# A new order of steps in the down stages of an mLSTM cell with a GELU feed-forward

## The chip, the cores and the metric

The kernel runs on one core of one Trainium2 chip. The metric is the device time of one execution in microseconds (us). Its engines are TensorE (PE), VectorE (DVE), ScalarE (ACT), GpSimd (POOL) and SyncE (SP), which here issues nearly all DMAs.

## The reference

Two parts follow each other. The first is a recurrent cell over 768 time steps for 4 batches and 8 heads of 40 elements; the second is a feed-forward block with exact GELU on the cell's output, 3072 rows of 320.

```python
for t in range(S):                                   # S = 768
    m_new = np.maximum(f_gate[:, :, t] + m, i_gate[:, :, t])
    f_stab = np.exp(f_gate[:, :, t] + m - m_new)
    i_stab = np.exp(i_gate[:, :, t] - m_new)
    m = m_new
    C = f_stab[..., None, None] * C + i_stab[..., None, None] * np.einsum('bhd,bhe->bhde', vt, kt)
    n = f_stab[..., None] * n + i_stab[..., None] * kt
    h_tilde = np.einsum('bhde,bhe->bhd', C, qt)
    denom = np.maximum(np.abs(np.einsum('bhd,bhd->bh', n, qt)[:, :, None]), 1.0)
    y[:, :, t] = sigmoid(o_gate[:, :, t]) * h_tilde / denom
x = y.transpose(0, 2, 1, 3).reshape(B * S, H * D)    # 3072 x 320
h = x @ w_in                                         # 320 x 2048
out = (0.5 * h * (1.0 + erf(h / sqrt(2)))) @ w_out   # 2048 x 320
```

## The kernel before

The sequence is cut into six chunks of 128 steps, numbered from 0. Within a chunk the cell becomes matmuls: scores of queries and keys times a matrix of decays, plus the state that the chunks before left. The feed-forward block of a chunk (512 rows: four batches of 128) has an up part (with GELU) and a down part.

The order of the work is written out by hand, as a string of words that `play` runs from left to right. Each word is a letter and batch numbers, and calls one Python function that emits instructions; each engine then runs its own instructions in that order, and an engine that has to wait holds all that is behind it on that engine. The string `FRONT` covers the start up to chunk 0's down part. The string `DOWN` is played once for each of the chunks c = 1 to 4: it mixes the down part of chunk c with the cell of chunk c+1. Between two plays of `DOWN` stands `up`, which is the same each time. Chunk 5's down part is written separately.

```python
steps = cell_steps(c + 1, "MWGTscVYXRLKQDCBSjh", g)
steps |= dict(F=in_turn(products), Z=in_turn(fourth[-1:]), N=late)
play(DOWN, steps)
```

The letters of `DOWN` mean this (b is a batch; numbers are lines):

- F: the next of 14 products of the down part (L1137). Each is 8 matmuls of 128x128 by 128x160 in full float32, which the trace shows as 16 matmul records. Seven results are made by two F each; after the second, the result leaves its bank: p1 (L1152) and p2 (L1158) by a ScalarE copy, p6, p5, p7, p3 and p4 by a VectorE addition (L1148). Two banks take turns.
- Mb, Wb: mask (POOL, L439) and exponential (ScalarE, eight of L465) of the matrix of decays W of batch b. Gb: the output gate (ScalarE sigmoid, L475). The exponential and the sigmoid lie in different activation tables, so a change between them puts a table load on ScalarE.
- S0, S2: the scores of batches 0 and 1, or 2 and 3 (TensorE, L557), and their multiplication with W (VectorE, eight of L563). C0, C2: what the state gives to the same two batches (L612). h0, h2: the state's update (TensorE L623, VectorE L632 and L638, POOL L636).
- Vb: the values (TensorE, L659) and their addition (VectorE, L667).
- Kb, Qb: VectorE transposes of keys and queries (L491) from blocks that a DMA brought. L3 clears and loads the block of batch 3 (POOL memsets L481, SP L167). D3: POOL product L528. B3: SP load of the last W. j: SP loads of the next chunk's first block (L167) and 16 copies from DRAM to DRAM (L159).
- Yb: the end of batch b (L674 to L688: ScalarE, POOL, VectorE) and, where its turn has come, a copy (L695). Xb: three transposes on TensorE into a bank px (L706) and a ScalarE copy (L716). Rb: two VectorE operations on px (L729, L730), after which the bank is free. Two px banks take turns.
- N: two VectorE subtractions (L1163) that the eleventh F and later ones need. Z: two VectorE subtractions of weights (L846), only in the first play.

```python
def sum_late():                                       # N
    for i in range(2):
        a12 = g.t[:, HF + HF // 2 * i:HF + HF // 2 * (i + 1), 0:HT]
        nc.vector.tensor_tensor(out=a12, in0=a12, in1=g.s2[i], op=OP.subtract)
```

Of the kernel before, what the change touches and what calls it, by code (L numbers as in the profile page):

```python
# [30 lines left out]
    M3 f2 S2 V1 Y0 T3 J Y1 C2 j8 W3 j9 e K K K J S3 J C3 f3 K X0 B8 J K R0 B9 h5 J h6 h7 K J V2 K Y2 J J Z Z K  # L31
    K V3 X1 J K r F J h8 h9 F F K F F F F F J K X2 G3 F F J K J F J K Y3 K B10 R1 X3 F p R2 J R3 F F J F F"""
DOWN = """
    M0 F Z F L3 W0 M1 W1 S0 C0 F F h0 Q2 F K2 G1 D3 B3 V0 G2 M2 W2 M3 W3 V1 K3 Q3 F G0 S2 Y0 G3 C2 h2 F
    F Y1 X0 V2 V3 F N F j R0 Y2 Y3 X1 F F X2 R1 F R2 X3 R3 F"""


@with_exitstack
# [1231 lines left out]
```

## Time and profile before

| what | value |
|---|---|
| median of 3 runs | 455.32 us (453.95 to 457.4) |
| the profiled execution | 455.19 us |
| its span, first to last instruction | 453.3 us |
| TensorE busy | 444.2 us (98%) |
| VectorE, ScalarE, POOL busy | 314.7, 238.2, 77.3 us |
| granted TensorE clock | 1.00 |
| DMA traffic | 51.12 MB, 113 GB/s over the span |
| TensorE's instruction transfers (queue q8) | 43 packets, 0.70 MB |

The profile is one execution. Busy times are unions of an engine's instructions; ends of matmuls are modelled, so TensorE can be shown busy while it makes less progress than it could. In a timeline line the first figure is the start in us, the second the duration of the merged group, and a bracket at the end names idle time ahead of it and what ended it. In a line that begins with a stretch A:B, the length comes first and then, for each engine, its busy time and number of instructions, the granted clock, the share of the DMA engines and GB/s. [...]

### The profile page before, as it was taken

The page shows a single profiled execution, that of the slowest core. Times are in us where ns is not written, and L with a number is a line of the kernel's source. Part 1 is how long each engine was busy: PE and PEld are TensorE (multiplying, and loading weights), DVE is VectorE, ACT ScalarE, POOL GpSimd, SP SyncE. Part 2 cuts the span into 40 slices and gives each one's busy share as a digit, 9 for nine tenths or more (in the row PEclk, how much of TensorE's full clock was granted, in tenths as well). Part 3 has the DMA queues.
Part 4 walks back from the last instruction along what each step waited for, and adds up shares of the span by engine and source line. Part 5 has one row for each costly group of instructions (what it writes and reads, how often), then busy time and mean ns, then how long its engine had stood idle before and what let it go on. Part 6 is the DMA issues. An engine that isn't in the chain of part 4 may idle for free.

```text
span 453.3 us, 13140 instructions
## 1 busy us (share of the span) xinstructions
PE 444.2 (98%) x5440; PEld 393.2 (87%) x5440; DVE 314.7 (69%) x672; ACT 238.2 (53%) x541; POOL 77.3 (17%) x117
## 2 busy tenths in 40 slices
PE   8899999999999999999999999999999999999996
PEld 7787888777788999988999988899988899988996
DVE  8797688877269688735578656488645577699940
ACT  4999999764231791221791203693203594247701
POOL 3002030000100443101433101533001513000000
PEclk9999999999999999999999999999999999999999
DMA  7999874886265644149834139942019930200001
GB/s 156 235 211 229 191 212 88 240 246 162 75 153 124 108 63 111 45 92 212 137 55 111 45 57 221 126 88 23 25 47 208 151 81 4 88 30 0 1 1 59
DMA packets 174876, 51.12 MB, mean 113 GB/s; under 512 B 154752, under 2 KB 168352, under 8 KB 174816
## 3 DMA queue, kind: packets, MB, share of 16 engines
q1 hardware_dynamic: 174496, 49.95, 50.5%
q8 instruction: 43, 0.70, 0.6%
q10 hardware_dynamic: 320, 0.33, 0.2%
q14 instruction: 17, 0.14, 0.1%
HBM read 45.47 MB, written 10.03 MB: 122 GB/s over the span
## 4 chain that ended last, share of the span: by engine, by line
PE 88%; ACT 6%; DVE 2%; DMA 1%; SPq 1%; issue 1%; DVEq 0%; ACTq 0%
PE po L1137 27%; PE pu L1021 23%; PE po L1116 8%; PE pu L1032 6%; PE po L991 6%; PE ph L659 3%; PE ps L557 3%; ACT W L465 2%; PE pu L810 2%; PE pf L612 2%; PE px L706 2%; PE pu L877 2%; PE pf L623 1%; SPq L151 1%; DMA bits<-in_moe_w_in_dram 1%
## 5 line engine op out<-in xcount | busy, mean ns | idle before, releaser
L1036 ACT ACTIVATE g<-pu 128x512 f32<-128x512 f32 x64 | 32.2, 618 | 81.2 <-PE pu L1032 81.2
L1137 PE MATMUL po<-w_out,g 128*128 128x160 f32 x512 | 74.4, 302 | 0.0
L1137 PEld LDWEIGHTS po<-w_out,g 128*128 128x128 f32 x512 | 70.1, 190 | 1.9 <-ACT g L1036 1.3
L1021 PE MATMUL pu<-x_hi,w_in_hi 128*128 128x512 f32 x160 | 39.0, 387 | 0.0
L465 ACT ACTIVATE W<-W,aT 128x128 f32<-128x128 f32 x128 | 38.6, 388 | 0.1
L439 POOL TENSOR_SCALAR_AFFINE_SELECT W<-W 128x1024 f32<-128x1024 f32 (+2 forms) x20 | 25.0, 1254 | 77.9 <-DMA W<-M_d 77.3
L1137 PE MATMUL po<-w_sums,sums 128*128 128x160 f32 x256 | 36.9, 302 | 0.0
L1137 PEld LDWEIGHTS po<-w_sums,sums 128*128 128x128 f32 x256 | 35.0, 190 | 0.4
L1116 PE MATMUL po<-w_out,g 128*128 128x320 f32 x128 | 34.9, 432 | 0.0
L1021 PEld LDWEIGHTS pu<-x_hi,w_in_hi 128*128 128x128 f32 x160 | 29.5, 189 | 5.7 <-ACT g L1036 1.3
L1116 PEld LDWEIGHTS po<-w_out,g 128*128 128x128 f32 x128 | 24.1, 190 | 9.7
L563 DVE TENSOR_TENSOR W<-ps,W 128x256 f32<-128x256 f32 (+1 forms) x48 | 18.1, 416 | 18.3 <-PE ps L557 7.1
L1021 PE MATMUL pu<-x_all,w_mid 128*128 128x512 f32 x80 | 30.3, 379 | 0.0
L1021 PE MATMUL pu<-x_all,w_in_mid 128*128 128x512 f32 x80 | 30.3, 379 | 0.0
L528 POOL TENSOR_TENSOR vw<-vb,ewT 128x328 f32<-128x328 f32 x12 | 9.2, 777 | 114.3 <-DMA vb<-in_v_dram 71.8
L864 DVE TENSOR_TENSOR sums<-g 128x512 f32<-128x512 f32 x16 | 12.8, 801 | 21.8 <-ACT g L1036 21.8
L384 DVE SCALAR_TENSOR_TENSOR pow<-sig,pow 128x320 uint32<-128x320 uint32 (+1 forms) x26 | 15.5, 597 | 7.2 <-ACT pow L373 7.2
L695 ACT COPY y_rest<-ob 128x128 f32<-128x128 f32 x16 | 4.7, 294 | 29.3 <-DVE ob L688 21.1
L372 ACT ACTIVATE sig<-bits 128x320 f32<-128x320 f32 (+1 forms) x26 | 15.1, 582 | 9.2 <-DMA bits<-in_moe_w_out_dram 4.4
L1021 PE MATMUL pu<-x_lo,w_in_lo 128*128 128x512 f32 x80 | 18.9, 379 | 0.0
L1021 PE MATMUL pu<-x_lo,w_in 128*128 128x512 f32 x80 | 18.9, 379 | 0.0
L1137 PE MATMUL po<-t,g 128*128 128x160 f32 x128 | 18.7, 299 | 0.0
(220 smaller groups left out, 960.8 us busy)
## 6 DMA issues: line engine op xcount, KB each, us to landing
W<-M_d SPq DMA_DIRECT2D x16, 512.0 KB, 5.2
bits<-in_moe_w_in_dram SPq DMA_DIRECT2D x20, 256.0 KB, 4.8
bits<-in_moe_w_out_dram SPq DMA_DIRECT2D x16, 320.0 KB, 4.5
blocks<-kq_d SPq DMA_DIRECT2D x32, 128.0 KB, 3.6
ob<-in_o_gate_dram SPq DMA_DIRECT2D x24, 160.0 KB, 4.6
out_dram<-o_sb SPq DMA_DIRECT2D x36, 80.0 KB, 1.9
kq_d<-in_k_dram SPq DMA_DIRECT2D x32, 80.0 KB, 2.4
kq_d<-in_q_dram SPq DMA_DIRECT2D x32, 80.0 KB, 2.5
```

The lines of the kernel that those rows point to most:

```text
L372: nc.scalar.activation(out=s, in_=hi.bitcast(F32), func=AF.Copy, scale=2.0 ** -112)
L384: nc.vector.scalar_tensor_tensor(out=p, in0=s, scalar=3, in1=p, op0=OP.logical_shift_left, op1=OP.bitwise_or)
L439: nc.gpsimd.affine_select(out=x, in_=x, compare_op=OP.is_ge, fill=1.0e30, base=base, pattern=[[0, H], [1, x.shape[2]]], channel_multiplier=-1)
L465: nc.scalar.activation(out=W[n][:, h, :], in_=src, func=AF.Exp, scale=-1.0, bias=aT[:, self.c, r:r + 1])
L557: nc.tensor.matmul(ps[i][hip][halves[x ^ i], p, t], kT[i][r, p, halves[x]], qT[i][r, p, t], start=True, stop=True)
L563: nc.vector.tensor_tensor(out=w[r, :, t], in0=ps[i][hip][r, :, t], in1=w[r, :, t], op=OP.mult)
L991: nc.tensor.matmul(in_pairs(po[t]), x[:, t * L:(t + 1) * L], in_turns(w), start=(f, k) == first, stop=(f, k) == last, skip_group_check=True)
L1021: nc.tensor.matmul(in_pairs(pus[i][e]), w[k][:, e, i * P:(i + 1) * P], in_turns(x[:, k, :]), start=(n == 0 and k == 0), stop=False, skip_g ...
L1032: nc.tensor.matmul(in_pairs(pu[e]), w[r, i // 2, i % 2 * P:(i % 2 + 1) * P], in_turns(x[r, NX, :]), start=False, stop=(n == 2), skip_group ...
L1036: nc.scalar.activation(out=g.t[:, HF * e + i, :], in_=pu[e], func=AF.Gelu, scale=4097.0)
L1116: nc.tensor.matmul(po[b], g.t[:, f, b * L:(b + 1) * L], w_out[:, f, :], start=(f == 0), stop=(f == NF - 1))
L1137: nc.tensor.matmul(bank[k][:, t, :], lhs(j, t), rhs(j), start=(first and t == 0 and j == 0), stop=(t == 1 and j == HF - 1), skip_group_che ...
```

## The change

The string `DOWN` is put in another order. It has the same words; nothing else in the program differs.

```diff
 DOWN = """
-    M0 F Z F L3 W0 M1 W1 S0 C0 F F h0 Q2 F K2 G1 D3 B3 V0 G2 M2 W2 M3 W3 V1 K3 Q3 F G0 S2 Y0 G3 C2 h2 F
-    F Y1 X0 V2 V3 F N F j R0 Y2 Y3 X1 F F X2 R1 F R2 X3 R3 F"""
+    L3 G1 M0 F W0 M1 F K2 W1 S0 C0 B3 F F M2 Z h0 Q2 D3 V0 V1 W2 F M3 W3 G2 G0 F j Q3 K3 S2 Y0 C2 h2 G3 F F Y1
+    X0 V2 V3 N F Y2 R0 X1 F Y3 X2 R1 R2 F X3 R3 F F F"""
```

Seen from TensorE the steps stand as follows (words of other engines left out):

```
before  F F S0 C0 F F h0 F V0 V1 F S2 C2 h2 F F X0 V2 V3 F F X1 F F X2 F X3 F
after   F F S0 C0 F F h0 V0 V1 F F S2 C2 h2 F F X0 V2 V3 F X1 F X2 F X3 F F F
```

On the other engines: L3 and G1 come first, ahead of the first mask and exponentials; K2 comes ahead of the second exponentials; the gates G2 and G0 stand together behind the last exponentials; M2, Z, B3 and j move; N stands ahead of the ninth F, and R0 ahead of X1.

## The prediction

> **What bounds the kernel now.** I read the busy table first, then the busy time of each engine in the four stretches that the change touches, then TensorE's and VectorE's timelines of one of them, and last the packets of the instruction queues.
>
> ```profile
> PE 444.2 (98%) x5440; PEld 393.2 (87%) x5440; DVE 314.7 (69%) x672; ACT 238.2 (53%) x541; POOL 77.3 (17%) x117
> q8 instruction: 43, 0.70, 0.6%
> 147.41:190.09 42.68, 42.57 (x814) 41.10 (x813) 32.34 (x70) 23.85 (x60) 16.29 (x22) 1.00 0.44 85
> 216.79:260.06 43.27, 42.70 (x814) 41.09 (x813) 31.42 (x68) 23.85 (x60) 15.13 (x22) 1.00 0.46 85
> 286.75:329.55 42.80, 42.68 (x814) 41.09 (x813) 31.36 (x68) 23.86 (x60) 14.44 (x21) 1.00 0.36 57
> 356.25:396.69 40.44, 40.39 (x751) 39.37 (x749) 29.48 (x60) 23.95 (x61) 12.67 (x15) 1.00 0.33 64
> ```
>
> The last four lines are the down stages that run beside the cells of chunks 2, 3, 4 and 5 (I call them stages 2 to 5): length, then TensorE's busy time and its matmul records. TensorE has almost no idle time, at full clock. An order can only win what these stages lose beyond their matmuls. But a busy figure hides short waits, because ends are modelled, so I measured each step from start to start.
>
> ```profile
> 221.33 1.57 PE L557 MATMUL ps<-qT,kT 64*64 64x128 f32 x64
> 223.74 4.61 PE L1137 MATMUL po<-w_sums,sums 128*128 128x160 f32 x32
> 229.03 2.44 PE L1137 MATMUL po<-w_out,g 128*128 128x160 f32 x16
> 231.40 1.67 PE L659 MATMUL ph<-vb,W 128*32 128x41 f32 x128
> 233.00 2.44 PE L1137 MATMUL po<-w_out,g 128*128 128x160 f32 x16
> 235.37 1.84 PE L557 MATMUL ps<-qT,kT 64*64 64x128 f32 x60
> 244.54 0.71 PE L659 MATMUL ph<-vb,g 128*32 128x41 f32 x52
> 245.76 0.34 PE L659 MATMUL ph<-vb,g 128*32 128x41 f32 x12 [0.51 <-issue]
> ```
>
> Two losses show in stage 3. Scores and reads (S0 C0) take 223.74-221.33 = 2.41 us the first time. The second time (S2 C2, to L623 at 238.16) they take 2.79; in stage 2 it is 3.04, in stage 4 2.96, in stage 5 2.41. And 52 records into the last batch of values TensorE stops: 0.71 us from start to start, released by nothing but issue. VectorE says why S2 is slow:
>
> ```profile
> 232.26 0.71 DVE L491 STREAM_TRANSPOSE qT<-blocks 128x512 f32<-128x512 f32 x1
> 232.89 0.67 DVE L491 STREAM_TRANSPOSE kT<-blocks 128x512 f32<-128x512 f32 x1
> 233.59 0.91 DVE L667 TENSOR_TENSOR far<-ph,far 128x328 f32<-128x328 f32 x2
> 234.41 0.70 DVE L491 STREAM_TRANSPOSE kT<-blocks 128x512 f32<-128x512 f32 x1
> 235.04 0.67 DVE L491 STREAM_TRANSPOSE qT<-blocks 128x512 f32<-128x512 f32 x1
> ```
>
> K3 and Q3 end at 235.71, when S2 has already begun (235.37); its matmuls of the second batch wait for them.
>
> **The change, part by part.** Times with a plus count from the start of stage 3 (216.79). No instruction is added except waits; 4 of ScalarE's 28 table loads go, and TensorE has 3 wait instructions fewer.
>
> (a) *Products beside each other.* F after other matmuls costs more than F after F: 16 records alone take 231.40-229.03 = 2.37, twice 4.74, while the pair at 216.79 takes 4.54. Behind h0 the order F, V0 V1, F becomes V0 V1, F F: 0.20 less in stages 2 to 4. In stage 5, 6.72+2.37 become about 4.45+4.54: 0.10. The tail has as many pieces as before. Sum -0.7, bounds -0.9 and -0.3.
>
> (b) *The wait in S2.* Now K2 comes ahead of the score multiplies, where VectorE sat idle 2.1 us for ScalarE, so one transpose (0.67) leaves the queue ahead of K3. G1 goes ahead of W0: ScalarE ends the gelus at +2.18, then table load 1.28, gate 0.47, load 1.28, so W0 starts at +5.3 (it was +6.4), the copy of p1 (0.43) comes between W0 and W1, and W1 ends at +10.4 instead of +11.2. K3 and Q3 so end 0.67+0.7 sooner, at +17.5. TensorE reaches S2 at +18.25 (h0 ends at +12.24, values 1.47, F F 4.54). The wait falls away with 0.7 to spare; in stage 2 the weight sums that Z moved behind W1's multiplies take 0.55 of that. Of the excess of 1.56 in all, 0.27 (stages 2 and 4) lies in the C2 part and is not this wait. I take -1.2; bounds -1.3 and -0.6.
>
> What else moves is covered. POOL's two memsets of L3 (0.94 each, from +0.0, held until the up stage has read x_lo) now stand ahead of mask M0, which ends near +3.0; W0 needs it at +5.3. The p1 copy is 3 us later; its bank is next written by the fifth F, at +13.7. The p2 copy waits for W3 (mask M3 ends near +15.3, exponentials to +17.9, load 1.28, gates 0.83, copy 0.40: +20.4), and the seventh F wants that bank at +21.4: 1.0 to spare. On SP, the 20 issues of j stay held by Q2 as before (233.67 to 249.52), and the sends behind them begin at 255.92. B3 keeps its place on SP between L3's loads and those of V0. The table load that goes (1.28 per stage) lies on ScalarE, busy 23.9 of 43.
>
> (c) *Instruction transfers.* In the packet records the 16 KB packets of q8 come once in 256 TensorE instructions (43 for some 10,975). In the stop the packet moved from 243.18 to 244.33, TensorE went on at 245.76, 1.43 after its end, and the next packet began at 247.57. So a block that nothing runs ahead of costs a cycle of 4.39; the closest two starts are 3.43 apart (162.54, 165.97). The stop marks a block's start; from there I count 256 at a time, each F being 32 instructions, V0 V1 256, h0 64, S0 C0 256. By step rows, the blocks of the new order that run short are: stage 3, from the end of the F F behind C0 through h0 into V1, 0.74+1.1 = 1.9 us (it was 4.1, with an F inside); stage 3, the last F into V3, 2.4 (was 2.65, the one that stopped); stage 5, F into V1, 2.6 (was 4.6); stage 2, into C2, 2.7 as before; stage 4, 3.7 as before, and one of 2.2 becomes 4.2. The 1.9 looks worst, but its transfer is asked for while slow products are still queued: in the trace the packet there began at 226.97, ended at 228.12, plus 1.43 is 229.55, and TensorE needs the block at 223.74+4.54+0.74+1.1 = 230.1. The V3 stop stays: that block and the one ahead of it sum to 7.9 in both orders. I take 0.7 there and 0.5 elsewhere, against about 1.0 now: +0.2, bounds -1.0 and +6.7 (below).
>
> The Trainium skill, "Runtime: NRT & Kernel Launch", section "Instruction fetch mechanics", gives TensorE room for 2048 instructions, so that the cost of a boundary is mostly hidden. The stop at 245 speaks against it; by it this term would be zero in both kernels and the sum -1.6.
>
> (d) *The px banks.* X1 and X2 now stand one F earlier, N still ahead of them on VectorE. From V3's end: the add of L667 and N take until +3.1 (246.03 to 249.11 in the trace), reciprocal and gate product to +3.8, R0's two operations to +4.75; only then is X0's bank free for X2, whose place on TensorE is F, X1, F = 2.27+0.33+2.20 = +4.8. X3 behind R1 comes out as level. No slack: I take 0.1 in three stages, +0.3; bounds 0 and +3.6 (0.9 in each stage, as when L866 took 1.58 instead of 0.68 beside a POOL mask).
>
> Sum: -0.7-1.2+0.2+0.3 = -1.4. The profiled execution took 455.19 (span 453.3 and 1.9 around it), the median is 455.32; the forecast is 453.9 by either.
>
> **The rivals.** *All transfers hide* (0.20): the V3 stop goes too and nothing new waits: -0.7-1.3-1.0 = -3.0, 452.3. For it: blocks ahead of the short ones grow (stage 2, 3.2 to 5.2); against it: the 7.9 above. *The banks decide* (0.14): N's length puts X2 and X3 behind, about 0.45 to 0.9 a stage: -1.7+1.8 to -1.7+3.6, 455.4 to 457.2. For it: VectorE's operations stretch beside POOL; against it: POOL has one short product there. *A transfer is not asked for early* (0.09, the slower side): if a request goes out only when TensorE itself begins the block, the short blocks cost 4.39 less their length: 2.5, 2.0, 1.8, 1.7 and 0.7, 8.7 in all, against 1.0 now. With (a) and (b) that is +5.8: 461.1. It decides once the block of 1.9 has its transfer later than 0.6 us behind today's place. For it: fast blocks are packed closer; against it: the start at 226.97, 0.8 ahead of TensorE's own crossing. *The order does nothing* (0.05): another operation, such as the masks, holds K3 and Q3, and the time stays at 455.3.
>
> **How the numbers follow.** The forecast has 0.52, with its own range of 452.9 to 455.0. The range 452.0 to 456.6 adds the first rival, the last, and the lower half of the banks. Over 1% is 4.6 us, about what a measurement of this kernel tells from no change. All that these stages lose is 3.3 us, so faster by over 1% has 0.04, for what I cannot see; slower by over 1% has 0.10, the third rival and a little; the rest, 0.86, is within.
>
> **What would show it.** Stage lengths of about 42.2, 42.8, 42.4 and 40.5; S2 C2 at 2.4 in all; K3 and Q3 ending ahead of S2; a stop left in V3 of stage 3. A stop in V0 V1 of stage 3 over 0.5 us means (c) is wrong; X2 or X3 starting later than the end of the F ahead of it means (d). A stage over 43.3 makes the forecast wrong.

## The result, and the profile after

The changed kernel is slower: 459.53 us in the median of 8 runs (458.28 to 461.33) against 456.31 for the kernel before in the same session (8 runs, 453.95 to 457.4). The ratio (of the means) is 1.0086, with a 95% interval of 1.0058 to 1.0113. The profiled execution took 459.5 us with a span of 457.4. I had forecast 453.9 and a range that ended at 456.6: the sign was wrong.

The first line below is the busy table of the profile after; the others are the four down stages, in the same view and columns as those shown of before (length, then busy time and number of records of TensorE, its weight loads, VectorE, ScalarE and POOL, then clock, DMA share and GB/s).

```profile
PE 444.8 (97%) x5440; PEld 393.1 (86%) x5440; DVE 321.8 (70%) x672; ACT 232.8 (51%) x537; POOL 82.3 (18%) x117
148.09:191.75 43.66, 42.81 (x814) 41.02 (x813) 34.55 (x70) 22.48 (x59) 18.56 (x23) 1.00 0.43 83
218.45:262.44 43.99, 42.72 (x814) 40.94 (x813) 33.18 (x68) 22.48 (x59) 17.38 (x23) 1.00 0.44 84
289.15:331.60 42.45, 42.16 (x815) 40.81 (x813) 32.15 (x68) 22.46 (x59) 18.66 (x22) 1.00 0.35 58
358.25:400.75 42.50, 40.86 (x749) 39.44 (x748) 30.24 (x60) 26.80 (x69) 13.17 (x16) 1.00 0.35 69
```

Three things are to be seen. The stages sum to 172.60 us instead of 169.19, so 3.4 of the 4.1 us by which the span grew lie in them. The up stages between them last 26.69 us in both kernels, and what follows the last one 56.6; the rest lies ahead of the first stage, where the programs are alike and where the first stage began anywhere between 147.4 and 149.3 us in the profiles of this study. From here on I therefore compare sums of the four stages, and medians only beside them. Second, TensorE's idle time grows (43.99-42.72 = 1.3 us in stage 3, 1.6 in stage 5). Third, VectorE has *more* busy time (33.18 instead of 31.42 in stage 3), though it has the same 68 instructions.

Measured from start to start and added up over the four stages, TensorE's steps come to this:

| step of the prediction | forecast | measured |
|---|---|---|
| (a) F, up to V3 | -0.7 | -0.6 |
| (b) S0 C0 and S2 C2 | -1.2 | -0.9 |
| (c) values V (instruction transfers) | +0.2 | +2.0 |
| (d) from V3 on: X, F (px banks) | +0.3 | +2.95 |
| sum | -1.4 | +3.4 |

The gains came; two losses are far larger than I had them. TensorE's timeline of stage 3 shows both:

```profile
229.95 0.81 PE L623 MATMUL pf<-vw,kb 128*40 128x41 f32 x32
230.69 1.32 PE L659 MATMUL ph<-vb,W 128*32 128x41 f32 x91
232.51 0.57 PE L659 MATMUL ph<-vb,W 128*32 128x41 f32 x37 [0.50 <-issue]
...
250.07 2.34 PE L1137 MATMUL po<-w_out,g 128*128 128x160 f32 x16
252.65 0.41 PE L706 MATMUL px<-ident,ob 128*128 128x128 f32 x2 [0.24 <-DVE x_all L730]
...
253.01 2.34 PE L1137 MATMUL po<-w_out,g 128*128 128x160 f32 x16
255.67 0.41 PE L706 MATMUL px<-ident,ob 128*128 128x128 f32 x2 [0.32 <-DVE x_all L730]
```

V0 V1 stop after 91 records for nothing but issue (0.70 us from start to start; in stage 5, 1.32). X2 and X3 wait for L730, the second operation of R0 and R1, which empties their bank: F, at 2.18 us otherwise, takes 252.65-250.07 = 2.58 and 255.67-253.01 = 2.66 until the transposes start. In the kernel before, X3 follows its F without a wait:

```profile
255.49 2.34 PE L1137 MATMUL po<-t,g 128*128 128x160 f32 x16
257.67 0.38 PE L706 MATMUL px<-ident,ob 128*128 128x128 f32 x2
```

The timelines of POOL, VectorE and SP in stage 3 show what stands behind the first stop. The sums of the up stage's results (L864 to L866, hidden work of VectorE) now run beside all four instructions of the three masks M0 to M2 (POOL, L439), where only the two of M1 ran before. After the change:

```profile
220.44 5.66 POOL L439 TENSOR_SCALAR_AFFINE_SELECT W<-W 128x1024 f32<-128x1024 f32 x4
```
```profile
221.02 1.58 DVE L866 TENSOR_TENSOR g<-g 128x512 f32<-128x512 f32 x1
222.52 1.57 DVE L864 TENSOR_TENSOR sums<-g 128x512 f32<-128x512 f32 x1
224.12 1.02 DVE L865 TENSOR_TENSOR sums<-sums,g 128x512 f32<-128x512 f32 x1
225.07 1.57 DVE L866 TENSOR_TENSOR g<-g 128x512 f32<-128x512 f32 x1
```
```profile
226.79 0.38 SPq L184 DMA_DIRECT2D g<-M_d  x1
```

The same in the kernel before:

```profile
218.77 2.69 POOL L439 TENSOR_SCALAR_AFFINE_SELECT W<-W 64x1024 f32<-64x1024 f32 x2
```
```profile
219.36 1.58 DVE L866 TENSOR_TENSOR g<-g 128x512 f32<-128x512 f32 x1
220.86 1.13 DVE L864 TENSOR_TENSOR sums<-g 128x512 f32<-128x512 f32 x1
222.03 0.69 DVE L865 TENSOR_TENSOR sums<-sums,g 128x512 f32<-128x512 f32 x1
222.64 0.69 DVE L866 TENSOR_TENSOR g<-g 128x512 f32<-128x512 f32 x1
```
```profile
223.47 0.38 SPq L184 DMA_DIRECT2D g<-M_d  x1
```

B3's load (L184: 512 KB) waits for them, because its target is freed by them. It was issued at 223.47-216.79 = +6.7 of the stage and is now issued at 226.79-218.45 = +8.3. The packet of 16 KB that holds the end of V0 V1 began, by the packet records, at +10.18 before (226.97). Now it begins at 230.24, +11.8, as the burst of B3's load fades (DMA engines full from 228.2 to 229.5), it ends at 231.22, and TensorE goes on 1.29 us later.

My theory: (1) the tail loses 2.9 us to the px banks, because N and the end of batches 2 and 3 stand ahead of R0 and R1 on VectorE while X2 and X3 have moved forward; (2) V0 V1 lose 2 us because the masks slow the sums, the sums delay B3's load, and that load's burst delays an instruction packet. The rival to (2): the stops come simply from putting h0, V0 and V1, all fast work, next to each other. The rival to (1): N, or the chain that ends batches 2 and 3, holds the tail wherever X2 stands.

### The profile page after: what moved, and what is told of

It reads as the page before. It is cut to its first block, busy times and chain, and to the rows that moved or that the text cites. A ratio compares the mean times of both kernels' runs of the same rounds, so it can differ in the third digit from the quotient of the medians.

```text
span 457.4 us, 13122 instructions
## 1 busy us (share of the span) xinstructions
PE 444.8 (97%) x5440; PEld 393.1 (86%) x5440; DVE 321.8 (70%) x672; ACT 232.8 (51%) x537; POOL 82.3 (18%) x117
## 4 chain that ended last, share of the span: by engine, by line
PE 74%; issue 11%; DVE 7%; ACT 5%; POOL 2%; DVEq 0%; POOLq 0%; ACTq 0%
PE pu L1021 23%; PE po L1137 19%; PE po L1116 8%; PE po L991 6%; PE pu L1032 6%; PE ph L659 3%; PE pu L810 2%; PE ps L557 2%; DVE g L1163 2%; ACT W L465 2%; PE pf L612 1%; PE px L706 1%; POOL ob L679 1%; ACT g L1036 1%; PE pu L877 1%
## 5 line engine op out<-in xcount | busy, mean ns | idle before, releaser
L439 POOL TENSOR_SCALAR_AFFINE_SELECT W<-W 128x1024 f32<-128x1024 f32 (+2 forms) x20 | 27.7, 1398 | 55.5 <-DMA W<-M_d 40.0
L528 POOL TENSOR_TENSOR vw<-vb,ewT 128x328 f32<-128x328 f32 x12 | 9.1, 771 | 117.9 <-DMA vb<-in_v_dram 30.2
L864 DVE TENSOR_TENSOR sums<-g 128x512 f32<-128x512 f32 x16 | 14.6, 910 | 21.8 <-ACT g L1036 21.8
L1148 DVE TENSOR_TENSOR o_sb<-po,o_sb 128x320 f32<-128x320 f32 x20 | 9.8, 491 | 18.5 <-PE po L1137 18.3
L481 POOL MEMSET blocks<- 32x1024 f32 x8 | 7.6, 945 | 74.7 <-PE pu L1032 74.5
L372 ACT ACTIVATE sig<-bits 128x320 f32<-128x320 f32 (+1 forms) x26 | 15.1, 581 | 10.2 <-DMA bits<-in_moe_w_out_dram 6.3
L1021 PE MATMUL pu<-x_lo,w_in_lo 128*128 128x512 f32 x80 | 18.9, 379 | 0.0
```

The lines of the kernel that those rows point to most:

```text
L372: nc.scalar.activation(out=s, in_=hi.bitcast(F32), func=AF.Copy, scale=2.0 ** -112)
L439: nc.gpsimd.affine_select(out=x, in_=x, compare_op=OP.is_ge, fill=1.0e30, base=base, pattern=[[0, H], [1, x.shape[2]]], channel_multiplier=-1)
L864: nc.vector.tensor_tensor(out=s1, in0=a21, in1=a22, op=OP.add)
L1021: nc.tensor.matmul(in_pairs(pus[i][e]), w[k][:, e, i * P:(i + 1) * P], in_turns(x[:, k, :]), start=(n == 0 and k == 0), stop=False, skip_g ...
```

## The experiments

Each edit is of the string `DOWN` of the changed kernel unless said; only the words around it are shown. "Sum" is that of the four stages in one profile (before 169.19, changed 172.60). The sizes of stops differ between profiles: the three kernels with the same words up to V3 (changed, old tail, N behind R0) stop in V0 V1 for 0.70, 0.42 and 0.71 us in stage 3 and for 1.32, 1.32 and 1.60 in stage 5. So a difference of 0.3 us between two sums shows nothing by itself.

| kernel | sum, against before | ratio to before (95%) |
|---|---|---|
| changed | +3.4 | 1.0086 (1.0058 to 1.0113) |
| masks moved | +2.1 | 1.0043 (1.0023 to 1.0063) |
| old tail | -0.3 | 1.0018 (0.9994 to 1.0041) |
| an F back between h0 and V0 | +2.3 | 1.0050 (1.0029 to 1.0071) |
| small B3 | +1.5 | 1.0036 (1.0015 to 1.0057) |
| N behind R0 | +2.2 | 1.0056 (1.0036 to 1.0075) |
| masks moved, N behind R0 | +0.8 | 1.0030 (1.0014 to 1.0046) |
| before with K2 early | -0.5 | 0.9984 (0.9967 to 1.0000) |
| three repairs | -0.8 | 0.9993 (0.9978 to 1.0008) |
| two orders | -2.0 | 0.9961 (0.9944 to 0.9979) |

1 us is a ratio of 0.0022. By that every sum lies in the interval of its ratio, the old tail's at the very edge: its sum is 0.3 us below that of before and its ratio 0.8 us above, so whether that kernel is faster or slower than the one before stays open.

### Masks moved

```diff
-L3 G1 M0 F W0 M1 F K2 W1 S0 C0 B3 F F M2 Z h0 Q2 D3 V0 V1
+M0 L3 G1 F W0 M1 F K2 W1 S0 C0 B3 F F Z h0 M2 Q2 D3 V0 V1
```

> The changed kernel (median 459.5, 0.9% over the kernel before) with two words of its order moved: M0 goes back ahead of L3, and M2 goes behind h0, so that POOL's masks no longer run back to back beside VectorE's hidden sums (L864 to L866, which took 1.57, 1.02 and 1.57 us there where 0.69 had been usual). Theory 1 (the masks slow the sums, B3's 512 KB load goes out 1.7 us later, and the instruction packet of the block h0 V0 V1 waits behind that load's burst): the sums of stage 3 end near +6.5 us instead of +8.2, the packet of that block is back ahead of +14, the stops inside V0 V1 (0.70 us in stage 3, 1.32 in stage 5) fall under 0.2, and S2's wait of 0.47 us in stage 2 goes; the waits of X2 and X3 stay. Stages about 43.2, 43.2, 42.4 and 41.0, in all 2.3 to 2.8 us less: about 457. Theory 2 (the stops come from putting h0, V0 and V1 next to each other, whatever B3 does): both stops stay at their size, and the time goes down by 0.5 us at most, 459.

In stage 3 (from 217.85) the mask that is left there (M1) and the sums, from the timelines of POOL and VectorE:

```profile
219.84 2.69 POOL L439 TENSOR_SCALAR_AFFINE_SELECT W<-W 64x1024 f32<-64x1024 f32 x2
```
```profile
221.93 1.13 DVE L864 TENSOR_TENSOR sums<-g 128x512 f32<-128x512 f32 x1
223.09 0.69 DVE L865 TENSOR_TENSOR sums<-sums,g 128x512 f32<-128x512 f32 x1
223.70 0.69 DVE L866 TENSOR_TENSOR g<-g 128x512 f32<-128x512 f32 x1
```

The sums end at +6.5 again, the packet begins at 228.19 (+10.3), and the stop in stage 3 is gone (V0 V1 1.67 instead of 2.32). VectorE's busy time over the whole kernel falls from 321.8 to 314.6 us, which is what it was before the change (314.7). So the masks cause the slow sums. But the stop in stage 5 only shrinks, from 1.32 to 0.86, and S2's wait in stage 2 stays (0.43 instead of 0.47). The gain is 1.3 us by the stages, 2.0 by the ratios, less than the 2.3 to 2.8 expected: the theory holds for stage 3 and only for part of stage 5, and S2's wait in stage 2 has another cause.

### The old tail

```diff
-V2 V3 N F Y2 R0 X1 F Y3 X2 R1 R2 F X3 R3 F F F
+V2 V3 F N F R0 Y2 Y3 X1 F F X2 R1 F R2 X3 R3 F
```

> The changed kernel's order up to V3, and the kernel before's order from there (F N F R0 Y2 Y3 X1 F F X2 R1 F R2 X3 R3 F). Theory 1 (N and Y2 stand ahead of R0 on VectorE while X2 comes one F earlier, so X2 and X3 wait for the px banks): the gaps ahead of X2 and X3, ended by L730, of 0.97, 0.88, 0.38 and 0.55 us in the four stages go, the stops inside V0 V1 stay, and the time goes down by 2.8 us: about 456.7. Rival (the end of batches 2 and 3, Y2 and Y3, or N itself holds the tail whatever the place of X2): gaps of the same sum show up ahead of X2, X3 or the eleventh F with another releaser, and the time stays at 459.5 within 0.8.

TensorE's tail in stage 3, with no idle time left:

```profile
256.08 0.38 PE L706 MATMUL px<-ident,ob 128*128 128x128 f32 x2
256.30 0.27 PE L706 MATMUL px<-ident,y_rest 128*128 128x128 f32 x1
256.40 2.34 PE L1137 MATMUL po<-t,g 128*128 128x160 f32 x16
258.58 0.38 PE L706 MATMUL px<-ident,ob 128*128 128x128 f32 x2
```

From V3's end to the end of the stage it is 14.04 us in each of the four, as before the change, against 15.06, 14.98, 14.45 and 14.62 in the changed kernel. The tail alone is worth 2.95 us, and the rival falls. The stop in stage 5 stays at 1.32, so it has nothing to do with the tail. The sum falls by 3.7: the other 0.7 lies in the values of stage 3, whose stop in V0 V1 is 0.42 here and whose V2 V3 take 1.49 instead of 1.89, with the same words ahead of them.

### An F back between h0 and V0

```diff
-h0 Q2 D3 V0 V1 W2 F M3 W3 G2 G0 F j
+h0 Q2 D3 F V0 V1 W2 M3 W3 G2 G0 F j
```

> The changed kernel with one F put back between h0 and V0 (h0 Q2 D3 F V0 V1 ... G2 G0 F, as the kernel before had it); masks, sums and B3 stay as the change has them. Both theories expect the stops inside V0 V1 to shrink, since TensorE comes to the second half of the block some 2.3 us later: from 0.70 and 1.32 us to under 0.2, against 0.2 us a stage lost because the two F no longer follow each other: 458.0 to 458.6. If the stops only move into V0 V1 one F later at the same size, the block's length is not what sets them, and the time is 460.

Both stops are gone: V0 V1 take 1.60 us in stages 3 to 5, although the words of masks, sums and B3 stay where the changed kernel has them, and in stage 3 the packet begins at +11.80, as late as there. The (c) of the values falls from +2.0 to -0.6 against before. Of these 2.6 us only 1.1 are left in the sum: S2 C2 of stage 4, 2.41 us in the changed kernel, take 2.83 with a stop of 0.44 for issue inside C2, the two F that no longer follow each other cost 0.6 as in the kernel before, and the tail is 0.5 longer. So the length of the block counts as well: when TensorE needs the block later, the late packet hurts nobody.

### Small B3

```diff
-nc.sync.dma_start(out=to, in_=src.unsqueeze(0).to_broadcast([P, H, L]))
+nc.sync.dma_start(out=to[0:P // 8], in_=src.unsqueeze(0).to_broadcast([P // 8, H, L]))
```

> The changed kernel, with B3's load of the last W (L184) to 16 of the 128 partitions only, 64 KB instead of 512 KB; 7/8 of that load is left out, so one batch's W is made from old data on the other partitions. The sums on VectorE stay slow and late (they end near +8.2 us), and the order of all engines is that of the changed kernel. Theory 1 (the instruction packet of the block h0 V0 V1 waits behind the burst of B3's load on the DMA engines): the packet begins about 1 us earlier in stage 3 and 1.5 us earlier in stage 5, and the stops inside V0 V1 (0.70 and 1.32 us) fall under 0.2; the time goes down by 1.5 to 2.2 us: about 457.5. Theory 2 (the stops come from the packing of h0, V0 and V1 alone): packet and stops stay, 459.5 within 0.5.

TensorE's V0 V1 of stage 3, which begins at 218.00:

```profile
229.50 0.81 PE L623 MATMUL pf<-vw,kb 128*40 128x41 f32 x32
230.24 1.67 PE L659 MATMUL ph<-vb,W 128*32 128x41 f32 x128
```

The sums are as slow and as late as in the changed kernel (they end at 226.19, +8.2), V0 and V1 stand as close behind h0, only the burst is missing. The packet begins at 228.18, +10.18, where the kernel before had it, and the 128 records run through. So in stage 3 the packing alone makes no stop. In stage 5 the packet begins at +10.8 instead of +11.9, and the stop goes from 1.32 to 0.77: what is left is the packing's. The gain by the stages is 1.9 us.

The three runs together settle (c): a packed block (V0 V1 right behind h0) has no room for a late packet, and the late burst makes the packet late. Stage 3 needs both for a stop. In stage 5, which has no h0, the packing alone costs 0.77 here; the late burst makes it 1.32 to 1.60.

### N behind R0

```diff
-V2 V3 N F Y2 R0 X1 F Y3 X2
+V2 V3 F Y2 R0 N X1 F Y3 X2
```

> The changed kernel with N moved behind R0 (V2 V3 F Y2 R0 N X1 F Y3 X2 ...), nothing else. The run with the old tail has shown that the waits ahead of X2 and X3 belong to the tail; this one asks whether N is what holds R0. Theory 1 (N, two subtractions of about 1.3 us, stands ahead of R0 on VectorE, and X2 finds its bank taken): the gaps ahead of X2 in the four stages fall from 0.49, 0.40, 0.38 and 0.55 us to under 0.1, those of X3 likewise unless R1, now behind N, comes late; the time goes down by 1.5 to 2.8 us: 456.7 to 458. Rival (the wait only moves: the eleventh F, two F later, waits for N): a gap ahead of an F, ended by L1163, of 0.5 us or more in each stage, and the time stays at 459.5.

X2's waits are gone in all four stages (the F ahead of it takes 2.18), and no F waits for N. But X3's grow, to 0.79, 0.68, 0.27 and 0.03 us, as the end of TensorE's tail in stage 3 shows:

```profile
253.06 2.34 PE L1137 MATMUL po<-w_out,g 128*128 128x160 f32 x16
255.92 0.41 PE L706 MATMUL px<-ident,ob 128*128 128x128 f32 x2 [0.52 <-DVE x_all L730]
```

N held R0, as theory 1 says. Now it holds Y3, and Y3 holds R1: the waits in the tail fall only from 2.9 to 1.9 us.

### Masks moved and N behind R0

The two edits above together.

> Both repairs in the changed kernel: M0 ahead of L3 and M2 behind h0 (the run with the masks moved), and N behind R0. If the two causes are separate, the gains add: the stages of the run with the masks moved (43.62, 43.36, 42.41, 41.89) less the gaps of X2 and X3 that they still have (about 0.9, 0.8, 0.3, 0.4): 42.7, 42.6, 42.1, 41.5, in all 0.3 us less than the kernel before, so a ratio of 0.999 to 1.000. If they are one cause (a late VectorE), N behind R0 gains less than 1 us here and the ratio is 1.002 or more.

The stages are 43.3, 43.1, 42.3 and 41.3: against the run with only the masks moved, N gains 1.3 us by the stages, against the changed kernel it gained 1.3 as well. So the two causes add up, but neither repair is whole, and the ratio stays at 1.003, above the 0.999 to 1.000 expected: with X3 still waiting the tail loses 2.0 us, and the stop in stage 5 is still 0.58.

### K2 alone, in the kernel before

```diff
-L3 W0 M1 W1 S0 C0 F F h0 Q2 F K2 G1 D3
+L3 W0 M1 W1 K2 S0 C0 F F h0 Q2 F G1 D3
```

> The kernel before with one word moved: K2 ahead of S0, so that one transpose of 0.67 us leaves VectorE's queue ahead of K3. Step (b) of the prediction by itself. If K3 and Q3 end 0.67 us sooner and nothing takes the place of that wait, S2 C2 take 2.4 to 2.5 us in stages 2 to 4 instead of 3.04, 2.79 and 2.96, and the time goes down by 1.0 to 1.2 us: a ratio of 0.9975. Rival (VectorE has something else in front of K3, the transposes being late through W3 or the additions of the values): S2 C2 stay above 2.7 and the time stays the same.

In stages 3 and 4 S2 C2 take 2.41 us instead of 2.80 and 2.96: step (b) works as reasoned. In stage 2 they take 3.59 instead of 3.04. TensorE's timeline there:

```profile
166.20 1.57 PE L557 MATMUL ps<-qT,kT 64*64 64x128 f32 x64
167.58 1.09 PE L612 MATMUL pf<-state,qT 64*64 64x41 f32 x62
169.60 0.25 PE L612 MATMUL pf<-state,qT 64*64 64x41 f32 x2 [0.93 <-issue]
```

S2's wait has gone (64 records in 1.39 from start to start), and TensorE stops in C2 instead, two records before its end: it came to the end of its block about 0.5 us sooner, while that packet, with the DMA engines loaded from 166 to 169 us, began at +19.45 of the stage (167.17-147.72) instead of +18.56. That the load made it late was not tested here. So half of the gain of 1.1 us in the other two stages was paid back here.

### Three repairs together

K2, G1 and W0 as in the changed kernel, the masks moved, an F between h0 and V0, and the old tail.

> What the runs so far leave standing, together: the changed kernel's K2, G1 and W0 placed early, M0 back ahead of L3 and M2 behind h0, an F back between h0 and V0, and the kernel before's tail. By theory 1 no stop is left in V0 V1 (shown by the run with the F put back), none ahead of X2 and X3 (shown by the run with the old tail), and the sums end near +6.5 us: stages of about 42.5, 42.1, 42.0 and 40.5, 2.1 us less than the kernel before, a ratio of 0.9955. If the gains of the new order were never real (S2's wait, for one, only traded for the stops), the stages stay at 42.7, 43.3, 42.8 and 40.4 and the ratio is 1.000.

The stages are 42.7, 42.5, 42.7 and 40.4, the ratio 0.9993 with an interval that holds 1. The forecast failed by 1.3 us. Half of it is stage 4: the stop in C2 (0.52 us) that came with the F between h0 and V0 is back. Another 0.4 is stage 3, where V2 V3 take 1.91 us instead of 1.49, and 0.2 is stage 2. So far one order for all four stages repairs one and spoils another; that the boundaries of the blocks lie differently in each stage would explain it.

### Two orders

The last order for stage 5 only; for stages 2 to 4 the masks moved and the old tail, with V0 V1 directly behind h0.

```diff
-    play(DOWN, steps)
+    play(DOWN5 if c == 4 else DOWN, steps)
```

> Two orders instead of one. Chunks two to four take the changed kernel's head with the masks moved (V0 V1 directly behind h0) and the kernel before's tail; chunk five takes the order of the last run, with an F between h0 and V0. The runs so far show the stop in V0 V1 left only in the last of the four stages once the masks are moved, and the stops in C2 of chunk two and chunk four (1.16 and 0.52 us) only where an F stands between h0 and V0. If instruction transfers are a matter of how long each block of 256 takes and of what is on the DMA engines then, both kinds are avoided at once: stages of about 42.6, 42.4, 42.0 and 40.4, in all 167.4, 1.8 us less than the kernel before: a ratio of 0.996. If a stop that is avoided in one block always comes back in the next, the stages stay near 42.7, 42.5, 42.7 and 40.4 and the ratio at 0.999.

```profile
148.03:190.48 42.45, 42.25 (x814) 40.94 (x813) 33.18 (x70) 22.49 (x59) 16.27 (x22) 1.00 0.44 82
217.18:259.30 42.12, 42.07 (x814) 40.93 (x813) 31.85 (x68) 22.49 (x59) 16.03 (x22) 1.00 0.49 90
286.00:328.00 42.00, 41.89 (x814) 40.77 (x813) 30.73 (x68) 22.48 (x59) 16.35 (x21) 1.00 0.35 57
354.69:395.27 40.58, 40.46 (x751) 39.38 (x749) 29.64 (x60) 22.64 (x60) 11.70 (x15) 1.00 0.35 68
```

The sum is 167.15, 2.0 us less than before the change, and the ratio is 0.9961 (0.9944 to 0.9979), as forecast: faster than the kernel before by 0.4%, 455.05 us in the median against 456.85 for the kernel before in that session. Idle time in stages 3 to 5 is 0.05 to 0.12 us. What is left is S2's wait in stage 2 (S2 C2 still 3.04).

## Why the prediction was wrong

Two terms of the sum failed: (d), put at +0.3, measured +2.95, and (c), put at +0.2, measured +2.0. The gains of (a) and (b), put at -1.9, came to -1.5.

**(a) Products beside each other** was right: the F ahead of V3 take 0.2 us less in stages 2 to 4. In stage 5 they take 18.08 in both orders, so the 0.1 that I gave it was nothing.

**(b) The wait in S2** was right in kind and a quarter too large: -0.9. K3 and Q3 end at 235.99, +17.5 of stage 3, where the sum put them, and S2 C2 take 2.41 in stages 3 and 4:

```profile
235.32 0.67 DVE L491 STREAM_TRANSPOSE kT<-blocks 128x512 f32<-128x512 f32 x1
```

With the masks moved they end at 235.40, +17.55, so the slow sums do not touch this step. In stage 2 S2 C2 still take 3.04. The term that was too small is the weight sums that Z moved. I took 0.55; these are the lines of L846 in VectorE's timelines of the changed kernel and of the kernel before:

```profile
160.49 1.39 DVE L846 TENSOR_TENSOR t<-w_out,w_sums 128x160 f32<-128x160 f32 x2
```
```profile
153.87 0.55 DVE L846 TENSOR_TENSOR t<-w_out,w_sums 128x160 f32<-128x160 f32 x2
```

In stage 2 of the changed kernel, K3 then ends at 166.95, +18.9, behind the start of S2 (+18.3), and S2 waits for it:

```profile
166.28 0.67 DVE L491 STREAM_TRANSPOSE kT<-blocks 128x512 f32<-128x512 f32 x1
```
```profile
167.00 1.44 PE L557 MATMUL ps<-qT,kT 64*64 64x128 f32 x56 [0.20 <-DVE kT L491]
```

That is 1.3 later than in stage 3, where there is no Z. Moving the masks did not mend it; in the run with K2 alone, where Z keeps its old place, S2 of stage 2 does not wait. That Z causes the wait is read from these lines; Z was not moved by itself.

**(c) Instruction transfers** failed at the sentence "its transfer is asked for while slow products are still queued". The asking was right: without the burst the packet begins at +10.18, as before. What I did not ask was what else is on the DMA engines then. In the trace of before, B3's 512 KB were issued at 223.47 and had landed some 3.6 us later, and the packet began at 226.97: there was no room between the two. I had written that B3 keeps its place between the loads on SP; its place in the queue is not its time, since it waits for VectorE's sums. And "what else moves is covered" left out that POOL's masks slow VectorE: the four instructions of M0 to M2, 5.66/4 = 1.4 us each on average, now stand beside the sums, which costs the last three 4.16-2.51 = 1.65 us more than before (1.57+1.02+1.57 against 1.13+0.69+0.69). For stage 5 the block of 2.6 was judged harmless beside the one of 1.9. It was the worse one: 0.8 with the packing alone, 1.3 with the burst. The sum that cleared the block of 1.9 was not made for it. In the trace of before, the packet that runs ahead of V0 V1 in stage 5 began at 367.30 (+11.05) and ended at 368.29; with 1.43 more it would serve TensorE at +13.47. In the new order TensorE comes to that point at 371.13, +12.88. That is a stop of 0.6 us by estimate, without any burst.

The Trainium skill states the lock behind the slow sums, in "SBUF — State Buffer", section "SBUF: two separate sides": VectorE's operations with two SBUF inputs and GpSimd's operations that read SBUF share a pair of ports, which one of them holds for a whole instruction. The trace agrees: the first sum beside POOL's memsets, which read nothing, took 0.69, and those beside masks up to 1.58. I had such a row, 1.58 beside a mask, as a bound of (d), and did not carry it to the sums.

**(d) The px banks** was the mechanism named, mis-sized tenfold: 0.3 against 2.95 us, near the bound of 3.6. X2 lost about 1.8 us of it, in all four stages, and X3 about 1.0, in stages 2 and 3. For X2 the times were nearly right: R0 ended +5.0 after V3 in stage 3 (252.51-247.47) where I had +4.75, since N's first subtraction took 1.74 us instead of 1.42, and the place of X2 was +4.8. The step that failed is the price of "no slack": 0.1 in three stages for what is lost in every stage, each tenth of lateness with the release on top (0.14 us from the end of L730, 252.51, to the start of X2). X2 came 0.38 to 0.55 late. For X3, "comes out as level" failed. The lines of VectorE in the changed kernel's stage 3:

```profile
251.08 0.49 DVE L688 TENSOR_TENSOR ob<-ob,den 128x320 f32<-128x320 f32 x1
...
253.59 1.01 DVE L688 TENSOR_TENSOR ob<-ob,den 128x320 f32<-128x320 f32 x1 [0.54 <-POOL ob L679]
254.52 0.55 DVE L729 SCALAR_TENSOR_TENSOR x_lo<-px,x_hi 128x384 fp32r<-128x384 f32 x1
254.98 0.54 DVE L730 TENSOR_TENSOR x_all<-px,x_hi 128x384 fp32r<-128x384 f32 x1
```

Ahead of R1 stands Y3. Its last product (253.59) waits 0.54 for POOL and then takes 1.01 instead of 0.49 beside another POOL product (L528, 253.51 to 254.25); in the kernel before it had taken 1.01 as well (254.20). POOL in turn had waited for ScalarE, whose first operation of Y3 (252.25 to 252.46) stood behind the copy of Y2's result, which waited for N. (POOL's row, at 252.54, names L730, which ended at 252.51; I read ScalarE from the tile that it needs.) I had counted Y2 and not Y3.

**The rivals.** "The banks decide" came true as described, 0.4 to 1.0 us a stage, and had 0.14. "A transfer is not asked for early" named the condition that did decide, a packet over 0.6 us behind its old place, but with another cause (a load in front) and at a quarter of the price: 2 us and not 7.7 (8.7 less 1.0). I had treated the two as alternatives. They came together, with the gains of (a) and (b) beside them: -0.6-0.9+2.0+2.95.

Still open is why the packet of stage 5 begins at +10.8 even without the burst, although TensorE comes to V0 at +11.5, sooner than in stage 3 (packet +10.2, V0 at +12.2; all four in the run with the small B3). It is no effect of the change: in the kernel before it began at +11.05, and an F ahead of V0, which began at +13.7 there, kept it from being felt.

## What to carry to other kernels

When a program is reordered on an engine without idle time, look at every other engine for what the new neighbours do to each other: a POOL operation can double the time of VectorE's beside it, and a load that waits for VectorE then lands on the transfer of instructions. A sum that ends with no slack is a loss, and must be charged with the spread of its rows, for each buffer and each operation ahead of it. Where the repetitions of a stage stop at different places, one order for all is a compromise; two orders gained what none of the single ones did.

## What the runs showed of the hardware

- VectorE's 128x512 sums take 0.69 us alone and up to 1.58 beside POOL's masks, but 0.69 beside POOL's memsets; moving the masks away took 7.2 us off VectorE's busy time (321.8 to 314.6).
- A 16 KB instruction packet that comes due during a 512 KB load began as the load's burst faded (+11.1 to +11.8 in stage 3 of four kernels), and at +10.18 with that load cut to 64 KB; where TensorE waited for a packet, it went on about 1.3 to 1.5 us after its end (231.22 to 232.51 in the changed kernel, 369.30 to 370.75 with the masks moved).
- A stop for instructions wanders: taken out of one block it came back in another, 1.16 us in C2 of stage 2 where, with K2 alone moved, a wait of 0.5 had been removed ahead of it.
